# Centring instead of normalising three token tiles before the K and V projections, and moving two tile transposes from TensorE to DMA

## The chip, the cores and the metric

The kernel runs on one core of a Trainium2 chip. The metric is the time of one execution on the device in microseconds (us), as a median of several executions. The profile covers the kernel's own span, which is about 1.8 us shorter than that time.

## The reference, cut to what matters

```
xn  = layernorm(x)                       # x: 2048 tokens x 1024, no gain, no bias
q, k, v = xn @ wqkv                      # 32 heads of 32
phi(t) = where(t > 0, t + 1, exp(t)) + 1e-6
kv = sum over tokens of phi(k) v ;  z = sum over tokens of phi(k)
s  = (phi(q) kv / (phi(q) z + 1e-6)) @ wo
g  = silu( (silu(xn @ w_gate) * (xn @ w_up)) @ w_down )      # inner width 3584
out = x + s * g
```

The tokens are cut into 16 tiles of 128. The projections of this kernel take a tile with the model dimension on the partitions (the first axis of a tile, 128 long), so each normalised tile is transposed before K and V are projected from it.

## The kernel before

The kernel goes through stages: K and V of all tiles with the running state (up to about 128 us), Q and the attention result, and then the feed-forward part, which takes the most time. Only the first stage is rewritten. For each tile `i` the code has these helpers (shortened, `...` marks a cut):

```
NPE = 4                                   # tiles 0..3 are transposed by TensorE
def emit_stats(i): ...                    # VectorE: mean and variance
def emit_rstd_act(i): ...                 # ScalarE sqrt + VectorE reciprocal (tiles 0, 1)
def emit_rstd(i): ...                     # three small VectorE operations + Newton steps on GpSimd
def emit_N(i):                            # (x - mean) * rstd
    ...
    if i >= NPE:                          # ... and for tiles 4..15 the transpose, by DMA
        nc.sync.dma_start_transpose(out=xn_ap(...), in_=xn[:])
def emit_TR(i):                           # tiles 0..3: 8 TensorE transposes of 128x128, then a copy from PSUM
    ...
def emit_Bmm(i, c):                       # K (c = 0, 1) and V (c = 2, 3): 8 matmuls 128x512 into one PSUM bank
    ...
def emit_Bev(i, c):                       # K: ScalarE Exp and Relu, VectorE; V: ScalarE copy
    ...
def emit_C(i):                            # 8 matmuls: add tile i to the state
```

They are called in a fixed order, which is the order of instructions on each engine:

```
wps = psB.tile([P, CW], FP32, name="warm_ps", tag="B")          # psB has three PSUM banks
for k in range(NWARM):                                          # 11 matmuls on zeros
    nc.tensor.matmul(wps[:], lhsT=warm[:, 0:P], rhs=warm[:], start=True, stop=True)
emit_stats(0); emit_rstd_act(0); emit_N(0); emit_TR(0)
emit_stats(1); emit_rstd_act(1); emit_N(1)
emit_Bmm(0, 0); emit_TR(1); ...
```

PSUM is the memory in which the matmuls leave their results; here one result of 128x512 fills a bank. The loads of x and of the weights, and all transposing DMAs, are issued from one queue (SyncE) in program order. In the built program each transfer on it waits for the completion of the one eight before it.

Of the kernel before, what the change touches and what calls it, by code (L numbers as in the profile page):

```python
# [9 lines left out]
ACT = mybir.ActivationFunctionType  # L10
ALU = mybir.AluOpType
# [10 lines left out]
def kernel(  # L22
# [34 lines left out]
    NJ = (G + GPT - 1) // GPT  # L57
    EPS_LN = 1e-5
    EPS = 1e-6
    NPE = 4  # L60
    NWARM = 11
    NPREP = 13
    NWE = 7
# [37 lines left out]
    ident = persist.tile([P, P], BF16, name="ident")  # L101
    make_identity(nc, ident[:])
    ones = persist.tile([P, P], BF16, name="ones")
    nc.vector.memset(ones[:], 1.0)
    mkp = p12.enter_context(tc.tile_pool(name="mkp", bufs=1, reuse_waits="tile"))
    mask = mkp.tile([P, P], FP32, name="mask")
    nc.vector.memset(mask[:], 0.0)
    for j in range(HPG):
        nc.vector.memset(mask[j * DH:(j + 1) * DH, j * DH:(j + 1) * DH], 1.0)
    sel = mkp.tile([P, HPG], FP32, name="sel")  # L110
    nc.vector.memset(sel[:], 0.0)
    for j in range(HPG):
        nc.vector.memset(sel[j * DH:(j + 1) * DH, j:j + 1], 1.0)

    xn_blk_tiles = {b: xnp.tile([P, DC, TB], BF16, name="xnT", tag="xn8")
                    for p in range(NB // 2 - 1, -1, -1) for b in (2 * p, 2 * p + 1)}

    def xn_ap(dcs, tok):
        b = tok.start // TB
        return xn_blk_tiles[b][:, dcs, tok.start - b * TB:tok.stop - b * TB]  # L120
# [3 lines left out]
    wq_sb = w12.tile([P, DC, D], BF16, name="wq_sb")  # L124
    late = p12.enter_context(tc.tile_pool(name="late", bufs=1, reuse_waits="tile"))
    KVZ = late.tile([P, G, NDW], BF16, name="KVZ")
    s_dram = dram.tile([S, D], BF16, name="s_dram")
    HK = DC // 2
    TB2 = 2 * TB
# [12 lines left out]
        while phi_late:  # L142
            phi_late.pop(0)()

    def emit_phi(work, t_ps, dst, W, in_place=False, act=False):
        e_t = work.tile([P, W], FP32, name="e_t", tag="e_t")
        if act:
            nc.scalar.activation(out=e_t[:], in_=t_ps, func=ACT.Relu, scale=-1.0)
            nc.scalar.activation(out=e_t[:], in_=e_t[:], func=ACT.Exp, scale=-1.0)
            nc.scalar.activation(out=t_ps, in_=t_ps, func=ACT.Relu)  # L150
            phi_late.append(lambda: nc.vector.scalar_tensor_tensor(out=dst, in0=e_t[:], scalar=EPS, in1=t_ps,
                                                                   op0=ALU.add, op1=ALU.add))
            return
        nc.scalar.activation(out=e_t[:], in_=t_ps, func=ACT.Exp)
        if in_place:
            r = t_ps
            nc.vector.tensor_scalar(out=r, in0=t_ps, scalar1=0.0, scalar2=EPS, op0=ALU.max, op1=ALU.add)
        else:
            r_t = work.tile([P, W], FP32, name="r_t", tag="r_t")
            r = r_t[:]  # L160
            nc.scalar.activation(out=r, in_=t_ps, func=ACT.Relu)
            nc.vector.tensor_scalar(out=r, in0=r, scalar1=EPS, scalar2=None, op0=ALU.add)
        nc.vector.scalar_tensor_tensor(out=dst, in0=e_t[:], scalar=1.0, in1=r,
                                       op0=ALU.min, op1=ALU.add)
# [198 lines left out]
    with ExitStack() as p1:  # L363
# [39 lines left out]
        load_x(0)  # L403
        load_x(1)
        load_wkv(0, halves=2 if DC % 2 == 0 else 1)
        load_x(2)
        nx = 3
        for c in range(1, NCH):
            load_wkv(c)
        for i in range(nx, NT):  # L410
            load_x(i)
        def load_qo(wt, wv, c):
            nc.sync.dma_start(out=wt[:, :, c * CW:(c + 1) * CW], in_=wv[:, :, c * CW:(c + 1) * CW])

        for c in range(NCC):
            load_qo(wq_sb, wqkv_v, c)
        PRE_AT = {2: (5, 6), 3: (7, 8), 4: (9, 10), 5: (11, 12), 6: (13, 14), 7: (15,)}
        FMAX = nc.vector.BN_STATS_FMAX
        SCH = min(FMAX, D)
# [4 lines left out]

        grp_state = {}

        N_AT = {5: (4,), 6: (5,)}
        for k in range(6, NT):
            N_AT[k + 3] = (k,)

# [33 lines left out]
        def emit_rstd(gid, eng=None):  # L464
# [10 lines left out]
            for _ in range(NR_ITERS):  # L475
# [3 lines left out]
                                  op0=ALU.mult, op1=ALU.add)  # L479
                eng.tensor_tensor(out=y, in0=y, in1=w[:, 0:n], op=ALU.mult)  # L480

        def emit_norm(i, dst, cols=None):
            mv, rstd, k = ln_state[i]
            src = x_ap(i) if cols is None else x_ap(i)[:, cols]
            return nc.vector.tensor_scalar(out=dst, in0=src, scalar1=mv[:, k, 0:1], scalar2=rstd[:, k:k + 1],
                                           op0=ALU.subtract, op1=ALU.mult)
# [3 lines left out]
        def emit_N(i):  # L490
            xn = xnw.tile([P, D], BF16, name="xn", tag="xn")
            xn_tiles[i] = xn
            if i < 2:
                for hh in range(2):
                    cols = slice(hh * (D // 2), (hh + 1) * (D // 2))
                    emit_norm(i, xn[:, cols], cols=cols)
            else:
                emit_norm(i, xn[:])
            ln_state.pop(i)
            if i >= NPE:  # L500
                xn_tiles.pop(i)
                nc.sync.dma_start_transpose(out=xn_ap(slice(0, DC), slice(i * P, (i + 1) * P)), in_=xn[:])

        def emit_TR(i):
            tok = slice(i * P, (i + 1) * P)
            xn = xn_tiles.pop(i)
            nh = 2 if i < 2 else 1
            dch = DC // nh
            for hh in range(nh):
                tr_ps = psC.tile([P, dch, P], BF16, name="tr_ps", tag="C")  # L510
                for dc in range(dch):
                    nc.tensor.transpose(tr_ps[:, dc, :], xn[:, (hh * dch + dc) * P:(hh * dch + dc + 1) * P], ident[:])
                dst = xn_ap(slice(hh * dch, (hh + 1) * dch), tok)
                if i == 1 and hh == 0:
                    nc.vector.tensor_copy(out=dst, in_=tr_ps[:])  # L515
                else:
                    nc.scalar.copy(out=dst, in_=tr_ps[:])  # L517

        pkv_tiles = {}

        kv_banks = {}

        def emit_Bmm(i, c):
            tok = slice(i * P, (i + 1) * P)
            kv_ps = psB.tile([P, CW], FP32, name="kv_ps", tag="B")
            kv_banks[(i, c)] = kv_ps
            for dc in range(DC):
                mm = nc.tensor.matmul(kv_ps[:], lhsT=xn_ap(dc, tok), rhs=wkv_sb[:, dc, c * CW:(c + 1) * CW],  # L528
                                      start=(dc == 0), stop=(dc == DC - 1))
                if dc == 0 and c == 0:  # L530
                    marks[("B", i)] = mm

        def emit_Bev(i, c):
            kv_ps = kv_banks.pop((i, c))
            if i not in pkv_tiles:
                pk_sb = work.tile([P, D], BF16, name="pk_sb", tag="pk_sb")
                pkv_tiles[i] = (pk_sb, v_bufs[i % 2])
            pk_sb, v_sb = pkv_tiles[i]
            if c < NCC:
                emit_phi(phiw, kv_ps[:], pk_sb[:, c * CW:(c + 1) * CW], CW, in_place=i >= 9)  # L540
            else:
                vc = c - NCC
                nc.scalar.copy(out=v_sb[:, vc * GPC:(vc + 1) * GPC, 0:P],
                               in_=kv_ps[:].rearrange("p (g c) -> p g c", c=P))

        def emit_C(i):
            pk_sb, v_sb = pkv_tiles.pop(i)
# [7 lines left out]
        def ln_pre(i, eng=None):  # L555
            emit_stats(i)
            if i == grp_tiles(i)[-1]:
                emit_rstd(grp_of(i), eng)

        warm = work.tile([P, CW], BF16, name="warm", tag="warm")  # L560
        nc.vector.memset(warm[:], 0.0)
        wps = psB.tile([P, CW], FP32, name="warm_ps", tag="B")
        for k in range(NWARM):
            nc.tensor.matmul(wps[:], lhsT=warm[:, 0:P], rhs=warm[:], start=True, stop=True)  # L564
        stat_ps[0] = lambda: psC.tile([P, 1], FP32, name="st_ps", tag="C")[:]
        emit_stats(0)
        emit_rstd_act(0)
        emit_N(0)
        emit_TR(0)
        emit_stats(1)  # L570
        emit_rstd_act(1)
        emit_N(1)
        emit_Bmm(0, 0)
        emit_TR(1)
        ln_pre(2)
        emit_Bev(0, 0)
        emit_Bmm(1, 0)
        emit_Bmm(0, 1)
        emit_Bev(1, 0)
        emit_N(2)  # L580
        emit_Bev(0, 1)
        emit_Bmm(1, 1)
        emit_Bmm(0, 2)
        emit_Bev(1, 1)
        emit_Bev(0, 2)
        emit_TR(2)
        emit_Bmm(1, 2)
        emit_Bev(1, 2)
        ln_pre(3)
        emit_Bmm(2, 0)  # L590
        emit_Bmm(0, 3)
        emit_Bev(0, 3)
        emit_Bmm(1, 3)
        emit_Bev(1, 3)
        emit_N(3)
        ln_pre(4)
        emit_C(0)
# [28 lines left out]
        for i in range(2, NT):  # L626
            for c in range(NCH):
# [10 lines left out]
                    emit_C(i - 1)  # L638
                emit_Bev(i, c)
                if (i, c) == (2, 2):  # L640
                    emit_TR(3)
                if c % 2 == 1:
                    for k in N_AT.get(2 * i + c // 2, ()):
                        emit_N(k)
                        if 0 <= k - NPE < NCC:
                            load_qo(wo_sb, wo_v, k - NPE)
                    for k in PRE_AT.get(i, ())[c // 2:c // 2 + 1]:
                        ln_pre(k)
                if (i, c) in PREP_AT:
# [785 lines left out]
```

## Time and profile before

| | before |
|---|---|
| time, three runs | 758.15 us (758.14 to 758.18) |
| span of the profiled execution | 756.7 us |
| first projection / tile 1's first projection | 7.60 / 10.24 us |
| first matmul of Q | 127.8 us |
| first matmul of the feed-forward part (output `xb`) | 245.3 us |

The profiled execution is one of 758.5 us, a little slower than the three runs.

The prediction below shows the page's head, the waits and the first 11 us. Two further views: the first is the timeline around tile 3's transpose on TensorE. Its columns are the start and the length in us, then engine, line, operation, output and input, and how many instructions are grouped.

```profile
29.15 0.61 PE L512 MATMUL tr_ps<-ident,xn 128*128 128x128 bf16 x8
29.60 3.62 PE L528 MATMUL kv_ps<-wkv_sb,xnT 128*128 128x512 bf16 x15
```

The eight transposes hold the stream from 29.15 to 29.60, which is 0.45 us, and the projections go on at once. That is what a tile's transpose costs on TensorE.

The second is the DMA view from 30 to 36 us. Each number is a slice of 0.15 us. It holds the kernel's first transposing DMA, that of tile 4, issued at 32.53. The lower row gives its time from issue to landing (3.2 us).

```profile
GB/s 348 341 362 335 362 335 301 198 116 41 27 20 27 20 27 20 7 0 55 0 0 0 0 0 0 55 205 213 222 207 208 210 179 169 105 92 191 130 116 307
...
xnT<-xn SPq DMA_TRANSPOSE x1, 3.2
```

About 1.25 us pass before the first bytes, the data take some 1.4 us at about 210 GB/s, and the rest of the 3.2 us is the time after the last bytes.

### The profile page before, as it was taken

What the parts mean: (1) busy time and instruction counts of PE and PEld (TensorE: products, weight loads), DVE (VectorE), ACT (ScalarE), POOL (GpSimd) and SP (SyncE); (2) the same over time, 40 slices, a digit from 0 to 9 for tenths busy, and PEclk for the clock granted to TensorE, in tenths of its full rate; (3) what the DMA queues carried; (4) which work ended last, traced back from release to release, by engine and by line L of the source; (5) the groups of instructions that cost most, each with busy time, mean ns of one, the idle gap of its engine ahead of it and who ended that gap; (6) DMA issues with size and microseconds to landing.
All of it is one profiled execution on the core that took longest, in us unless ns stands there. A gap on an engine that the chain in (4) does not pass through costs nothing.

```text
span 756.7 us, 10426 instructions
## 1 busy us (share of the span) xinstructions
PE 746.6 (99%) x3662; PEld 349.0 (46%) x3731; DVE 558.5 (74%) x1031; ACT 376.3 (50%) x526; POOL 278.4 (37%) x352
## 2 busy tenths in 40 slices
PE   8999999999999999999999999999999999999997
PEld 4544544454454444444444444444444444444443
DVE  6687787896697788888889775368676777787335
ACT  5677776889956565666659311132322223211122
POOL 2444799998540276868585000100000000200000
PEclk9999999999999999999999999999999999999999
DMA  9968799879679668878799236398644445530824
GB/s 316 295 149 146 223 334 300 302 137 307 201 180 298 229 217 292 309 268 312 278 329 408 86 121 239 124 377 321 229 174 167 167 168 173 180 133 15 283 83 135
DMA packets 105845, 170.30 MB, mean 225 GB/s; under 512 B 34816, under 2 KB 82176, under 8 KB 95168
## 3 DMA queue, kind: packets, MB, share of 16 engines
q1 hardware_dynamic: 100144, 144.99, 59.3%
q0 software_dynamic: 4208, 22.15, 7.5%
q10 hardware_dynamic: 1440, 2.49, 0.9%
q8 instruction: 29, 0.48, 0.3%
q14 instruction: 24, 0.20, 0.1%
HBM read 111.67 MB, written 50.59 MB: 214 GB/s over the span
## 4 chain that ended last, share of the span: by engine, by line
PE 97%; DVE 1%; ACT 1%; issue 1%; ACTq 0%; DVEq 0%
PE zw L939 26%; PE kv_ps L528 15%; PE xb L939 13%; PE dzw L1124 12%; PE yb L939 6%; PE q_ps L183 6%; PE dx L1124 6%; PE dy L1124 3%; PE fx L790 3%; PE s_ps L748 2%; PE kvz L550 1%; PE nd L717 1%; PE df L1124 1%; PE warm_ps L564 1%; DVE w_sb L283 0%
## 5 line engine op out<-in xcount | busy, mean ns | idle before, releaser
L939 PEld LDWEIGHTS <-w_sb 128*128 128x128 f16 (+1 forms) x1568 | 152.1, 98 | 182.7
L939 PE MATMUL xb<-xnT,w_sb 128*128 128x512 bf16 x420 | 113.3, 379 | 1.5
L528 PE MATMUL kv_ps<-wkv_sb,xnT 128*128 128x512 bf16 x499 | 112.9, 379 | 1.1 <-DVE xnT L515 0.3
L939 PE MATMUL zw<-xnT,w_sb 128*128 128x512 bf16 x448 | 105.8, 379 | 0.0
L939 PE MATMUL zw<-S,w_sb 128*128 128x512 f16 x448 | 105.8, 379 | 0.0
L295 POOL TENSOR_TENSOR w_sb<-w_sb 128x512 f16<-128x512 bf16 x42 | 50.2, 1195 | 95.7 <-DVE w_sb L283 51.3
L260 ACT ACTIVATE w_sb<-w_sb 128x2048 bf16<-128x2048 bf16 x42 | 79.9, 1902 | 4.4 <-DMA w_sb<-in_B_w_up_dram 4.4
L1124 PE MATMUL dx<-w_sb,hT 128*128 128x512 bf16 x202 | 76.6, 379 | 0.3
L528 PEld LDWEIGHTS <-xnT 128*128 128x128 bf16 x512 | 48.4, 98 | 55.9 <-ACT xnT L517 0.8
L1124 PEld LDWEIGHTS <-hT 128*128 128x128 bf16 (+1 forms) x462 | 44.7, 98 | 52.4
L183 PE MATMUL q_ps<-xnT,wq_sb 128*128 128x512 bf16 x249 | 58.0, 379 | 0.4
L1015 ACT ACTIVATE sg<-cg 128x1024 bf16<-128x1024 f32 x28 | 29.6, 1057 | 57.4 <-DVE cg L1008 57.4
L939 PE MATMUL yb<-S,w_sb 128*128 128x512 f16 x224 | 57.4, 378 | 0.1
L1124 PE MATMUL dzw<-w_sb,hT 128*128 128x512 f16 (+1 forms) x190 | 57.0, 379 | 0.0
L1008 DVE SCALAR_TENSOR_TENSOR cg<-zw,rc_all,s 128x1024 f32<-128x1024 f32 x28 | 35.9, 1284 | 25.5 <-PE zw L939 13.8
L967 DVE SCALAR_TENSOR_TENSOR s<-yb,rc_all,s 128x512 f32<-128x512 f32 x42 | 31.5, 749 | 28.1 <-ACT s L966 28.1
L296 POOL TENSOR_TENSOR w_sb<-w_sb 128x512 f16<-128x512 bf16 x42 | 50.5, 1201 | 3.3
L1064 POOL TENSOR_TENSOR hs<-hT 128x512 f16<-128x512 bf16 x2 | 2.5, 1250 | 132.6 <-ACT sg L1015 132.6
L298 POOL TENSOR_TENSOR w_sb<-w_sb 128x512 f16<-128x512 bf16 x42 | 50.2, 1196 | 0.0
L297 POOL TENSOR_TENSOR w_sb<-w_sb 128x512 f16<-128x512 bf16 x42 | 50.2, 1195 | 0.0
L1098 POOL DMA_DIRECT2D out_dram<-io x16 | 8.7, 542 | 101.9 <-DVE io L1097 101.6
L966 ACT ACTIVATE s<-xb,rcl 128x512 f32<-128x512 f32 x14 | 9.6, 687 | 65.3 <-PE xb L939 65.3
(179 smaller groups left out, 1187.4 us busy)
## 6 DMA issues: line engine op xcount, KB each, us to landing
w_sb<-pk_g SPq DMA_DIRECT2D x27, 1024.0 KB, 6.3
pk_g<-w_sb SPq DMA_DIRECT2D x14, 1024.0 KB, 5.0
w_sb<-wd SPq DMA_DIRECT2D x14, 1024.0 KB, 6.0
w_sb<-pk_u SPq DMA_DIRECT2D x14, 1024.0 KB, 5.0
pk_u<-w_sb POOLq DMA_DIRECT2D x13, 1024.0 KB, 5.3
w_sb<-wd SPq DMA_DIRECT2D x14, 768.0 KB, 4.8
w_sb<-in_B_w_gate_dram SPq DMA_DIRECT2D x14, 512.0 KB, 6.7
w_sb<-in_B_w_down_dram SPq DMA_DIRECT2D x28, 256.0 KB, 4.9
```

What stands on the lines that cost most here:

```text
L183: nc.tensor.matmul(q_ps[:], lhsT=wq_sb[:, dc, g * P:(g + 1) * P], rhs=xn_ap(dc, btok), start=(dc == 0), stop=(dc == DC - 1))
L260: nc.scalar.activation(out=junk, in_=raw_view(key, t), func=ACT.Square, accum_out=asum[:])
L295: nc.gpsimd.tensor_tensor(out=T1, in0=b12, in1=b11, op=ALU.subtract)
L296: nc.gpsimd.tensor_tensor(out=T2, in0=b22, in1=T1, op=ALU.subtract)
L297: nc.gpsimd.tensor_tensor(out=T3, in0=b22, in1=b12, op=ALU.subtract)
L298: nc.gpsimd.tensor_tensor(out=T4, in0=b21, in1=T2, op=ALU.subtract)
L528: mm = nc.tensor.matmul(kv_ps[:], lhsT=xn_ap(dc, tok), rhs=wkv_sb[:, dc, c * CW:(c + 1) * CW], start=(dc == 0), stop=(dc == DC - 1))
L939: mm = nc.tensor.matmul(out, lhsT=lhs(k), rhs=rhs(k), start=(first and k == 0), stop=(k == HK - 1), skip_group_check=True)
L967: nc.vector.scalar_tensor_tensor(out=s2[:], in0=y_[:], scalar=rc, in1=s1[:], op0=ALU.mult, op1=ALU.add)
L1008: nc.vector.scalar_tensor_tensor(out=d12, in0=zw[:], scalar=rc, in1=s2[:, None, :].to_broadcast([P, 2, TB]), op0=ALU.mult, op1=ALU.add)
L1015: nc.scalar.activation(out=sg[:, 1:3, :], in_=cf[:], func=ACT.Silu)
L1124: nc.tensor.matmul(out, lhsT=lhs, rhs=rhs, start=first, stop=lastk, skip_group_check=True)
```

## The change

It shortens the way to the first projection and takes work off TensorE.

- Tiles 0 to 2 are only centred for K and V. (x - mean) W times 1/std is the same as the projection of the normalised tile, and 1/std belongs to a token, which is a partition of the result. So 1/std can be the `scale` of the ScalarE instruction that empties the bank, and the projection doesn't wait for it.
- Tile 1's TensorE transposes go in halves between the projections of tile 0.
- Tiles 2 and 3 are transposed by DMA instead of TensorE.
- Q and the feed-forward part need the normalised tiles, so tiles 0 to 2 are normalised again later and transposed by DMA.
- x2 is loaded behind the second chunk of weights, x3 behind tile 2's transpose, and the loads of the Q weights are issued later.
- The warm-up reads other memory, whose memset comes first on VectorE, and writes two PSUM banks in turn.

```diff
-    NPE = 4
+    NPE = 2
+    NDF = 3
@@ phi and the V evacuation
-        nc.scalar.activation(out=e_t[:], in_=t_ps, func=ACT.Exp)
+        nc.scalar.activation(out=e_t[:], in_=t_ps, func=ACT.Exp, scale=scale)   # rstd_of[i] for i < NDF
...
@@ loads
-        load_x(2)
         for c in range(1, NCH):
             load_wkv(c)
-        for i in range(nx, NT):
-            load_x(i)
+            if c == 1:
+                load_x(2)
...
+        def emit_center(i):
...
+                nc.vector.tensor_scalar(out=xn[:, cols], in0=x_ap(i)[:, cols], scalar1=mv[:, k, 0:1], scalar2=None,
+                                        op0=ALU.subtract)
+            if i >= NPE:
+                emit_DT(i)
+        def emit_DT(i):
+            nc.sync.dma_start_transpose(out=xn_ap(slice(0, DC), slice(i * P, (i + 1) * P)), in_=xn_tiles.pop(i)[:])
...
-        wps = psB.tile([P, CW], FP32, name="warm_ps", tag="B")
+        wps = [psB.tile([P, CW], FP32, name="warm_ps", tag="B") for _ in range(2)]
@@ the order
         emit_stats(0)
+        emit_center(0)
         emit_rstd_act(0)
-        emit_N(0)
-        emit_TR(0)
+        emit_TR(0, 0, nc.scalar)
+        emit_TR(0, 1, nc.scalar)
         emit_stats(1)
+        emit_center(1)
+        emit_Bmm(0, 0, range(6))
+        emit_TR(1, 0, nc.vector)
         emit_rstd_act(1)
-        emit_N(1)
-        emit_Bmm(0, 0)
-        emit_TR(1)
+        emit_Bmm(0, 0, range(6, DC))
+        emit_TR(1, 1, nc.scalar)
...
+        emit_stats(2)
+        emit_center(2)
+        load_x(3)
...
+        for i in range(4, NT):
+            load_x(i)
...
+        emit_N(0)
         emit_N(3)
```

`emit_N(0)` normalises tile 0 again and issues its transposing DMA, which nothing needs before Q at about 128 us. `emit_N(3)` does the same for tile 3, which TensorE needs at about 29 us. The one for tile 0 stands first.

## The prediction

> **What bounds the kernel now.** I read the page's busy shares first, then the chain that ended last, then the waits of the matmul engine, then the first 34 us as a timeline. The first lines are from the page (busy us, share, count; then the chain's shares by engine).
>
> ```profile
> span 756.7 us, 10426 instructions
> PE 746.6 (99%) x3662; PEld 349.0 (46%) x3731; DVE 558.5 (74%) x1031; ACT 376.3 (50%) x526; POOL 278.4 (37%) x352
> ...
> PE 97%; DVE 1%; ACT 1%; issue 1%; ACTq 0%; DVEq 0%
> ```
>
> TensorE is busy for 746.6 of 756.7 us, and 97% of the chain is TensorE. So only two things pay: fewer TensorE instructions, or fewer gaps between them. Its whole list of waits above 0.2 us is four lines (us in total, times, longest):
>
> ```profile
> PE warm_ps L564 <- DVE warm L561: 1.5, 1, 1.5
> PE nd L264 <- ACT w_sb L260: 0.3, 1, 0.3
> PE kv_ps L528 <- DVE xnT L515: 0.3, 1, 0.3
> PE kv_ps L528 <- ACT xnT L517: 0.3, 1, 0.3
> ```
>
> Three of the four are in the first 11 us, the part that the change rewrites. The chain of waits there (start, us, what):
>
> ```profile
> 1.49 4.87 PE warm_ps L564 x11
> 6.36 0.57 PE tr_ps L512 x4
> 6.93 0.02 issue
> 6.96 0.59 ACT xnT L517
> 7.55 0.05 issue
> 7.60 1.90 PE kv_ps L528 x8
> 9.50 0.24 PE tr_ps L512 x4
> 9.74 0.02 issue
> 9.76 0.44 DVE xnT L515
> 10.20 0.05 issue
> 10.24 3.19 PE kv_ps L528 x14
> ```
>
> The 11 warm-up matmuls compute nothing, so the head is really paced by the statistics of token tile 0. The timeline shows these ahead of the first transpose (start, us, engine, what):
>
> ```profile
> 3.69 1.29 DVE L447 BATCH_NORM_STATS2 stats<-xp 128x6 f32<-128x512 bf16 x2 [1.47 <-DMA xp<-in_A_x_dram]
> 5.01 0.21 DVE L448 BATCH_NORM_AGGREGATE mv<-stats 128x2 f32<-128x12 f32 x1
> 5.32 0.29 ACT L460 ACTIVATE rstd<-mv,eps_ln 128x1 f32<-128x1 f32 x1 [3.29 <-DVE mv L448]
> 5.64 0.16 DVE L461 RECIPROCAL rstd<-rstd 128x1 f32<-128x1 f32 x1 [0.43 <-ACT rstd L460]
> 5.84 0.74 DVE L485 TENSOR_SCALAR xn<-xp,mv,rstd 128x512 bf16<-128x512 bf16 x2
> ```
>
> The trip to ScalarE and the reciprocal keep the normalisation from starting at about 5.26 (aggregate's end 5.22 plus a hop of 0.04); it starts at 5.84.
>
> **What the Trainium skill says.** (1) "TensorE: Matmul & The Clock Gate", Back-to-back issue gap, gives 55.6 and 215.7 ns between warm matmuls of 128 and 512 columns. The trace agrees: 8 transposes delay the stream by 0.45 us (56 ns each), and a group of 8 projections takes about 1.73 us (216 ns each). The 379 ns in the page's rows is latency, and I do not use it. (2) The same page, Part 1, has TensorE cold at half clock until some 3.4 us of activity. The warm-up spacing here, 0.43 us, agrees with a cold array, and the projections at 7.60 run at the warm rate. (3) "ScalarE: Activation LUTs", What ACT_TABLE_LOAD costs: each per-partition pointer operand adds about 93 ns. The trace has about 0.60 us for the Exp evacuation without a pointer and 0.67 for the one of s_ps, which has one; I take +0.07 to +0.09. (4) "Advanced Engine Details and Errata", X-Bar Transpose (TRN2), calls transposing DMAs as fast as regular ones. Here it is slower: around the first one (33.8 to 35.2 us) the queue moves some 210 GB/s, against about 385 when it loads x. So its 0.26 MB cost about 1.3 us of queue instead of 0.68.
>
> **The change, part by part.** *Start.* Centring needs only the mean, so it begins at 5.26 instead of 5.84: 0.58 us. The first half ends at about 5.63 and its transpose can start at 5.73, against 6.31. Warm-up must not be in the way: its memset now stands first on VectorE, so it starts 0.32 earlier (the memsets ahead of it took 0.84 to 1.16), and its last matmul gives way at about 5.7 to 5.9. I take 0.5 us of gain: first projection at 7.1 instead of 7.60.
>
> *Tile 1.* Its first transposes now go after 6 of the 8 projections of tile 0, its second after the last 2. VectorE: reciprocal 6.0, statistics 6.2 to 7.7, centring 7.75 to 8.5. TensorE: 6 projections 7.1 to 8.4, 4 transposes, copy on VectorE at about 8.4+0.42 = 8.82 to 9.25, meanwhile 2 projections and 4 transposes up to 9.35. So tile 1 starts at about 9.35 against 10.24: 0.9 in all up to here, which includes the 0.5.
>
> *Transposes of tiles 2 and 3.* 16 matmuls leave TensorE, 0.45 us per tile: 0.9 us. The wait on the copy of tile 3, about 0.1 ahead of its projections at 31.3, goes too.
>
> Sum: 0.9 + 0.9 + 0.1 = **1.9 us**. Tile 3 then starts at 9.35 + 8 groups x 1.73 + two state updates 1.07 + 3 x 1.73 = 29.4, against 31.3.
>
> *Added beside the path.* Tiles 0 to 2 are normalised again for Q and the feed-forward: 3 x 0.55 us on VectorE (74% busy) and three transposing DMAs, about 4 us of queue, at 21 to 35 us. The scaled evacuations are 18 x 0.08 = 1.4 us on ScalarE, half of it by 20 us. The wq loads move from 21 us to about 50, where the windows show the DMA at 50 to 79%, and Q reads them at 128. All of these have slack of tens of us, apart from the following.
>
> **The rivals.** *A. The DMA transpose of tile 3 comes late and takes the place of what was removed.* The queue is saturated from 2.4 to about 31 us in the trace before. Through weight chunk 3 it has the same 4.98 MB as before, whose last piece landed at 4.8 + 12.4 = 17.2. Then tile 2's transpose (1.3 us; data to 17.6), 13 x tiles (13 x 0.68 = 8.8, to 26.4), then the transposes of tile 0 (to 27.7) and tile 3 (to 29.1), landing at about 29.5. TensorE wants it at 29.4. This is a tie: I expect a stall between 0 and 0.8 us, and give 0.2 to the mean. The other way into it, tile 3's statistics, is: x3 lands 19, statistics and the three small operations to 20.7, the Newton steps on GpSimd 3.3 to 4.4 us, issue at 25 to 26; it is ahead of the queue's data. A stall over 2 us would need the queue to hold transposes much longer.
>
> *B. PSUM banks.* Three banks, freed by ScalarE after a table load of 1.28 us that cannot start before the last copy (10.57 before, 10.1 now): Exp 11.4, Relu to 12.6 or 12.7. The fourth group wants its bank at 9.35 + 2 x 1.73 = 12.8. There is a margin of 0.1, a tie again, worth at most 0.3. Later banks have 0.6, if x2 is not over a us late.
>
> *C. x2 and weight chunk 1.* Chunk 1 landed at about 2.75 + 8.4 = 11.15 before, with x2 in front of it; the second group of tile 0 now wants it at 11.1. Behind chunk 1, x2 (0.68 us of queue) lands at about 11.1 and chunk 1 at 10.4. So this part only prevents a new wait. Tile 2 is then centred at 13.3, transposed by about 18, and wanted at 23.2 - 1.73 = 21.4: 3 us of slack.
>
> *D. The gain is taken back later.* At 165 to 173 us the chain runs for a moment through weight preparation: DVE w_sb L283 (3.67 us), then ACT w_sb L260, with a TensorE wait of 0.3. If that ran on its own clock, up to 1.9 us would vanish. Against it: the chain enters that stretch from a TensorE matmul at 160.07, and every preparation step stands in program order between TensorE's evacuations, so it should shift with TensorE. After it no wait over 0.2 us is left up to the end.
>
> *E. The clock gate.* If the earlier, two-bank warm-up left the array cold for longer, some groups would run at 427 ns a matmul, 1.7 us lost a group. Little speaks for it: just as many warm-ups, and fewer gaps after them.
>
> **Range and chances.** 758.15 - 1.9 = 756.25. A costs 0.2 on average and B 0.05, so 756.5. With no stall and a hidden gap more it could be 755.9; with A at 1 us or D taking half, 757.5. 2% is 15 us; nothing here is that large in either direction.
>
> **What would show each step.** First centring at 5.2 to 5.3 and first projection at about 7.1; tile 1 at about 9.35; 16 fewer tr_ps matmuls; no TensorE wait on chunk 1; tile 2's first projection at 21.4; tile 3's at 29.4 to 30, with any wait put down to a DMA on xnT (A). Wait on ScalarE or a longer gap near 12.8 is B. Whether TensorE is still 1.7 to 1.9 us ahead at 128 us (first q_ps at 127.8 before) and after 175 us tells D. The prediction is wrong if the first stretch ends with less than 1 us gained, if a DMA transpose is over 1.5 us late, or if the lead at 128 us is not in the end time.

## The result, and the profile after

| | before | after |
|---|---|---|
| time, six runs of the same rounds | 758.14 us (758.00 to 758.19) | 758.65 us (758.07 to 759.74) |
| span of the profiled execution | 756.7 us | 756.3 us |
| tile 1's first projection | 10.24 us | 9.39 us |
| first matmul of Q | 127.8 us | 128.4 us |
| first matmul of the feed-forward part | 245.3 us | 245.2 us |

The ratio of after to before is 1.0008, with a 95% interval from 0.9995 to 1.002: no difference. Ratios here are the mean time of one kernel's runs over that of the other's runs of the same rounds, so they are not quite the ratio of the medians that I quote. The predicted 756.5 us, with a range from 755.9 to 757.5, is missed by 2.15 us. The profiled executions took 758.5 us before and 758.07 us after, which is the fastest of the six, so their spans differ the other way from the medians.

The page of the kernel after has these lines in place of those shown of before:

```profile
span 756.3 us, 10420 instructions
PE 745.0 (99%) x3647; PEld 348.0 (46%) x3715; DVE 558.2 (74%) x1034; ACT 376.1 (50%) x524; POOL 279.8 (37%) x352
...
PE 95%; DMA 2%; DVE 1%; issue 1%; POOL 0%; SPq 0%; ACT 0%
```

TensorE has fewer instructions and 1.6 us less busy time, as intended. (The count falls by 15 rather than 16; a few matmul records can be missing from a trace.) But the chain that ended last now runs through DMA for 2% of the span, where no DMA showed before. (By line, the page gives 2% to the loads of x that the statistics of a tile need, and 1% to a transpose, both rounded.) The waits of TensorE say what it costs:

```profile
PE kv_ps L533 <- DMA xnT<-xn: 1.6, 1, 1.6
PE warm_ps L569 <- DVE KVZ L118: 1.2, 1, 1.2
PE q_ps L186 <- ACT v_sb L549: 0.7, 1, 0.7
PE kv_ps L533 <- ACT xnT L519: 0.4, 1, 0.4
```

Before, no wait outside the first 11 us was longer than 0.3 us. Now there are two: 1.6 us for a transposing DMA and 0.7 us at the start of Q. The timeline of the kernel after shows how the first 34 us went:

```profile
5.17 0.61 DVE L489 TENSOR_SCALAR xn<-xp,mv 128x512 bf16<-128x512 bf16 x2
7.17 1.47 PE L533 MATMUL kv_ps<-wkv_sb,xnT 128*128 128x512 bf16 x6 [0.41 <-ACT xnT L519]
...
9.39 13.99 PE L533 MATMUL kv_ps<-wkv_sb,xnT 128*128 128x512 bf16 x63
...
13.31 1.34 SPq L495 DMA_TRANSPOSE xnT<-xn  x1
14.70 7.16 SPq L396 DMA_DIRECT2D xp<-in_A_x_dram  x13
...
22.29 12.27 SPq L495 DMA_TRANSPOSE xnT<-xn  x4
24.14 5.34 PE L533 MATMUL kv_ps<-wkv_sb,xnT 128*128 128x512 bf16 x23
...
31.07 1.90 PE L533 MATMUL kv_ps<-wkv_sb,xnT 128*128 128x512 bf16 x8 [1.59 <-DMA xnT<-xn]
```

Down to 24.14 everything is where the prediction has it. The 63 matmuls from 9.39 are unbroken, so tile 2, transposed by DMA, was not waited for. Then the group that starts at 24.14 ends, and tile 3 waits 1.59 us. The chain of waits of the kernel after names the transfer:

```profile
24.59 0.55 DVE xn L500
...
25.17 5.86 DMA xnT<-xn
31.02 0.05 issue
31.07 1.90 PE kv_ps L533 x8
```

Tile 3 is normalised at 25.14 and its transpose is issued at 25.17, inside the predicted 25 to 26. It then takes 5.86 us to land, nearly twice what the first transpose of the kernel before took on an idle queue. The DMA view from 26 to 30 us (slices of 0.1 us) shows what it waited behind:

```profile
GB/s 430 430 348 190 289 294 289 289 110 20 20 20 21 41 20 20 20 20 23 18 18 18 148 287 289 289 272 285 289 287 289 292 289 287 289 269 111 0 0 0
...
xnT<-xn SPq DMA_TRANSPOSE x1, 5.9
```

This row is read from left to right in four pieces. The x loads end at about 26.3, where the prediction had 26.4. Then data at another rate, some 290 GB/s, flow for half a microsecond: the first part of the transposes. From 26.9 to 28.2 almost nothing moves: about 20 GB/s, as in the tail of the kernel before, although two transposes are queued. From 28.2 to 29.7 both transposes move together at about 289 GB/s. Adding up the slices at 289 or so, before and after the pause, gives some 0.53 MB, which is just the two tiles of 0.26 MB each, so both tiles' data are through at 29.7. Even then tile 3's transfer counts as landed only at 31.02, 1.3 us later.

A sixteenth of the 350 to 390 GB/s that the loads reach is 22 to 24 GB/s. The Trainium skill ("DMA: Bandwidth & Descriptors", Why a DMA increments its semaphore by 16 and not by 1) says that a DMA runs on up to 16 engines that finish independently. So one engine of 16 that still works off its share of the loads would fit the 20 GB/s.

The views don't show this, but the packed trace of each run keeps sixteen landing signals for every transfer on this queue, and every packet. They agree. Up to the x load that landed at 22.20 the sixteen signals of a load come within 0.2 us. In each of the next six loads fifteen come together and one comes 1.4 to 1.5 us later: 22.87 and 24.34 in the first, 26.29 and 27.69 in the sixth. (All sixteen of the very last load come at 28.3 to 28.4.) The late part's packets of x go on to 27.9. The packets of the transposes stand still from 26.8 until then, and 22 of them took 1.4 us each, where some 18 ns is usual. Of tile 3's transpose fifteen parts have landed by 30.17, and the sixteenth comes at 31.02.

The lag of the x loads begins after a 16 KB transfer of the instruction queue, which took 1.09 us from 21.73; the one of tile 3 comes with an 8 KB transfer of such a queue at 29.6. The same order of events is in the profiles of all versions that send two transposes behind the x loads. That these transfers cause the lags fits, but no run moved them, so it is not shown.

### The profile page after: what moved, and what is told of

It is laid out like the page before. It is cut to its first block, busy times and chain, and to the rows that moved or that the text cites. A ratio compares the mean times of both kernels' runs of the same rounds, so it can differ in the third digit from the quotient of the medians. Undisturbed runs are those within 1.5% of the kernel's fastest.

```text
span 756.3 us, 10420 instructions
## 1 busy us (share of the span) xinstructions
PE 745.0 (99%) x3647; PEld 348.0 (46%) x3715; DVE 558.2 (74%) x1034; ACT 376.1 (50%) x524; POOL 279.8 (37%) x352
## 4 chain that ended last, share of the span: by engine, by line
PE 95%; DMA 2%; DVE 1%; issue 1%; POOL 0%; SPq 0%; ACT 0%
PE zw L953 26%; PE xb L953 13%; PE kv_ps L533 12%; PE dzw L1138 12%; PE q_ps L186 7%; PE yb L953 6%; PE dx L1138 6%; PE dy L1138 3%; PE fx L804 3%; PE s_ps L762 3%; DMA xp<-in_A_x_dram 2%; PE nd L731 1%; PE kvz L557 1%; DMA xnT<-xn 1%; PE df L1138 1%
## 5 line engine op out<-in xcount | busy, mean ns | idle before, releaser
L1029 ACT ACTIVATE sg<-cg 128x1024 bf16<-128x1024 f32 x28 | 29.6, 1057 | 57.5 <-DVE cg L1022 57.5
L981 DVE SCALAR_TENSOR_TENSOR s<-yb,rc_all,s 128x512 f32<-128x512 f32 x42 | 31.4, 748 | 30.2 <-ACT s L980 30.2
```

The costliest lines, as they stand in the source:

```text
L981: nc.vector.scalar_tensor_tensor(out=s2[:], in0=y_[:], scalar=rc, in1=s1[:], op0=ALU.mult, op1=ALU.add)
L1029: nc.scalar.activation(out=sg[:, 1:3, :], in_=cf[:], func=ACT.Silu)
```

## The experiments

The first question was whether tile 3's wait comes from the queue or from the tile's own statistics, and what it is worth. The second was what makes Q wait. The third, which came up on the way, was why some executions of the changed kernel end late although they were ahead at 245 us. The letters in the expectations are the rivals of the prediction and the names that the theories had. Edits are against the changed kernel unless I say otherwise. Every run gave correct results.

| run | what it is | median (range), us | ratio to before, 95% |
|---|---|---|---|
| e1_tile3_first | tile 3's DMA issued ahead of tile 0's | 758.19 (757.58 to 758.75) | 0.9998 [0.9985, 1.001] |
| e2_x_late | x8 to x15 loaded later | 759.29 (757.01 to 760.59) | 1.001 [0.9996, 1.0023] |
| e3_warm1 | one warm-up bank | 758.71 (758.44 to 759.13) | 1.0007 [0.9994, 1.0021] |
| e4_first_warm1 | e1 and e3 together | 757.12 (756.77 to 759.69) | 0.9991 [0.9978, 1.0003] |
| f1_first_warm3 | e1 with three warm-up banks | 757.21 (757.06 to 757.54) | 0.9987 [0.9974, 0.9999] |
| f2_warm3 | three warm-up banks alone | 759.03 (757.96 to 760.24) | 1.0008 [0.9995, 1.0022] |
| f3_after_again | the change, unedited | 758.34 (758.09 to 758.99) | 1.0002 [0.9989, 1.0014] |
| f4_tile3_pe | tile 3 back on TensorE | 757.00 (756.65 to 758.07) | 0.9985 [0.9972, 0.9997] |
| g1_pe3_warm3 | f4 with three warm-up banks | 756.88 (756.79 to 757.72) | 0.9984 [0.9972, 0.9997] |
| g2_x2_first | f1 with x2 ahead of weight chunk 1 | 756.51 (755.96 to 757.12) | 0.9979 [0.9965, 0.9992] |
| k1_g2_upfirst | g2, two later loads exchanged | 757.15 (756.59 to 758.49) | 0.9989 [0.9975, 1.0003] |
| k2_after_upfirst | the change, the same exchange | 758.70 (758.00 to 759.47) | 1.0004 [0.9991, 1.0016] |
| m1_before_dup5 | the kernel before, five DMAs twice | 758.91 (758.43 to 759.42) | 1.0005 [0.9992, 1.0019] |
| m2_g2_dup3 | g2, three DMAs twice | 757.36 (755.96 to 758.25) | 0.9985 [0.9973, 0.9998] |

Each of these is a median of five. The letter e, f, g, k or m marks what ran together on one chip; the kernel before had medians of 758.28, 758.13, 758.23, 758.33 and 758.33 beside them, of nine runs each.

### Is it the queue that makes tile 3 wait?

**e1_tile3_first** exchanges the order of the two transposing DMAs and nothing else.

```diff
-        emit_N(0)
+        emit_N(0, dt=False)      # normalise tile 0, no DMA yet
         emit_N(3)
+        emit_DT(0)
```

> The change, with tile 3's transposing DMA issued ahead of tile 0's (nothing else moved). Theory A (tile 3's transpose lands late because it stands behind the x loads and tile 0's transpose in one saturated queue; it landed at 31.0 us and TensorE wanted it at 29.4): tile 3's transpose lands some 1.3 us or more sooner, before 29.8, the TensorE wait of 1.6 us on it falls to 0.4 or less, tile 3's projections start at 29.4 to 29.9, and the time falls by 1.0 to 1.6 us against the change, if the later wait of 0.7 us on the last V evacuation stays. Rival I (the transpose is late because its own input is late: statistics and the Newton steps on GpSimd): its issue stays at 25.2 and it lands at 31 as before, no gain. Rival D (what is gained here is taken back later): tile 3 starts at 29.5, and the end still is within 0.3 us of the change.

The wait on tile 3 is gone. The timeline of this run has one unbroken group where the changed kernel had 23 matmuls and a wait:

```profile
24.37 7.34 PE L534 MATMUL kv_ps<-wkv_sb,xnT 128*128 128x512 bf16 x32
```

Tile 3's transpose is issued at 25.65 and lands after 4.1 us instead of 5.9. At 245 us this run is 1.2 us ahead of the changed kernel (243.97 against 245.21). Its end time gains less than the expected 1.0 to 1.6 us (758.19 against 758.65, in other rounds); a part of the reason comes below.

**e2_x_late** leaves the order as it is, and takes eight x loads out of the queue ahead of the two transposes.

```diff
-        for i in range(4, NT):
+        for i in range(4, 8):
             load_x(i)
...
         emit_N(3)
+        for i in range(8, NT):
+            load_x(i)
```

> The change, with the loads of token tiles 8 to 15 moved behind the transposes of tiles 0 and 3 in the queue. Theory A: the queue is short when tile 3's transpose is issued at 25.2, so it lands after about 3.2 us, at 28.4, the TensorE wait on it is gone, tile 3 starts at 29.4, and the time falls by about 1.6 us against the change; its spread over executions (758.07 to 759.74) shrinks to that of the kernel before (0.2 us). Rival I (late input): still issued at 25.2 and landing at 31, no gain. If A is right and a later statistics step now waits for x8 and later tiles, a new wait appears on VectorE after 36 us, with none on TensorE.

Tile 3 doesn't wait here either. The DMA view of this run from 22 to 29 us (slices of 0.175 us) shows the two transposes with nothing ahead of them:

```profile
GB/s 0 0 0 0 0 67 211 218 215 212 206 189 166 15 0 0 0 0 0 0 0 0 0 0 0 47 205 215 217 211 209 193 178 142 70 0 222 386 398 398
...
xnT<-xn SPq DMA_TRANSPOSE x2, 3.1
```

They are issued at 21.76 and 25.29 and land 3.1 us later. For the first, 1.2 us pass before the data, 1.4 us with data, and about 0.5 us after the last bytes (landing at 24.83). Tile 3 was normalised at 25.27, no earlier than in the changed kernel. So late input is not the reason; what differs is what the queue holds: 3.1 us with nothing ahead, 4.1 behind the x loads (e1), 5.9 behind the x loads and another transpose. The pause is absent here (in e1 the packets of the transposes still stand still for 0.6 us): all sixteen parts of the x loads ahead had landed by 21.73, before the first byte of a transpose. The version itself is no use. The later loads push back tile 4's transpose, and TensorE waits 1.48 us for that one at 38.2 and 0.44 us once more at 46.2, so the wait has only moved. The expected narrow spread didn't come either (757.01 to 760.59).

**f4_tile3_pe** gives tile 3 back to TensorE and keeps the rest of the change.

```diff
-        emit_N(3)
+        emit_N(3, dt=False)
...
                 if (i, c) == (2, 2):
                     emit_N(1)
+                    emit_TR(3, 0, nc.scalar)
+                    emit_TR(3, 1, nc.scalar)
```

> The change with tile 3 transposed by TensorE again (two halves, ScalarE copies), its DMA transpose dropped; all else as the change. Theory A: no wait on a DMA of xnT at tile 3, 0.45 us of transposes and up to 0.3 of waiting for the copy instead of 1.6: 0.8 to 1.2 us under the change. Rival D (nothing gained before 31 us reaches the end): no difference over 0.3.

It costs the 0.45 us of the eight transposes again and removes a wait of 1.6 to 1.9 us. Its median is 757.00, against 758.34 of the unedited change on the same chip (**f3_after_again**, where tile 3 waited 1.91 us): 1.3 us better, near the 1.45 us that 1.9 - 0.45 gives. The closeness is partly luck: in the profiles f4 is 1.0 us ahead of f3 at the first Q matmul (127.23 against 128.22), as it has a new wait of 0.47 us for a later tile's transpose at 44.6, and f3's profile has a late wait of 0.8 us at 328 us that f4's doesn't have.

> The change itself once more, for its spread and a second profile. If the late transpose of tile 3 is steady, the wait is again 1.3 to 2 us and the time 758.0 to 759.7. If the head is governed by the landing of x0 and of the second half of weight chunk 0 (0.4 to 0.7 us of wait in three of four experiments so far), the first projection and tile 1's start move by up to 0.8 us from the first profile.

### What makes Q wait?

In the changed kernel the first matmul of Q waits 0.68 us, with ScalarE's copy of the last V group ending just before. In the built programs the banks show why: with one or two banks taken by the warm-up, the rotation of the three banks puts the last V group of the stage into bank 3, and the first Q group wants just that bank. In the kernel before, the last V group is in bank 5. My first guess was that the second warm-up bank had shifted the rotation by one, so that one bank would put it right. **e3_warm1** tests that, and **e4_first_warm1** adds e1's order.

```diff
-        wps = [psB.tile(...) for _ in range(2)]
+        wps = [psB.tile(...) for _ in range(1)]
```

> The change, with the warm-up in one PSUM bank instead of two. Theory W (the second bank turns the rotation of three banks by one, so that the first Q group takes the bank that the last V evacuation is still reading): the TensorE wait of 0.7 us of the first q_ps on the V evacuation at 127.8 is gone, the head of the kernel is unchanged (first projection at 7.2, the wait on tile 3's transpose about 1.6), the time falls by 0.3 to 0.7 us. Rival (the wait comes from TensorE or ScalarE standing in another order, not from the bank): the wait of 0.7 stays.

> Both: tile 3's transpose ahead of tile 0's, warm-up in one bank. If A and W are right and their gains add: about 1.6 + 0.6 = 2.2 us off the change, some 756.3, that is 1.7 to 1.9 us below the kernel before, as the prediction's sum had it. Rival D: lead of 1.9 us at 127 us, but less than 1 us of it in the end time.

The guess was wrong: the Q wait is 0.7 us in both. (e3 waits 1.86 us for tile 3, and e4, with e1's order, 0.20 us, so that order alone leaves hardly any slack either.) The changed order of the projections had moved the rotation too. With three warm-up banks the built program has the last V group in bank 5 again. **f1_first_warm3** and **f2_warm3** do that, with and without e1's order.

> Tile 3's transpose ahead of tile 0's, warm-up in three PSUM banks. In the built programs the first Q group takes bank 3; the last V evacuation reads bank 5 in the kernel before, bank 3 in the change and in the variant with one warm-up bank (which is why that one kept the wait), and bank 5 in this variant. Theory W2 (same bank, so the first Q group waits for the evacuation): the wait of 0.7 us of q_ps on v_sb is gone, no wait above 0.3 us on tile 3's transpose, and the time is 0.6 us under that of e1_tile3_first: 757.0 to 757.6, or 756.5 if no new wait falls in. Rival (the order of the engines makes the wait): 0.7 stays.

> The change with three warm-up banks alone. W2: the wait of q_ps on v_sb gone, the wait on tile 3's transpose still 1 to 2 us; 0.6 us under the change: about 758.0. Rival: 0.7 stays, time as the change.

The wait disappears from both. The timelines of the changed kernel and of f1 around the start of Q:

```profile
127.76 0.60 ACT L549 ACTIVATE v_sb<-kv_ps 128x512 bf16<-128x512 f32 x1 [0.46 <-PE st_ps L267]
128.41 1.89 PE L186 MATMUL q_ps<-xnT,wq_sb 128*128 128x512 bf16 x8 [0.68 <-ACT v_sb L549]
```

```profile
125.71 1.02 PE L186 MATMUL q_ps<-xnT,wq_sb 128*128 128x512 bf16 x4
...
125.88 0.60 ACT L550 ACTIVATE v_sb<-kv_ps 128x512 bf16<-128x512 f32 x1 [0.46 <-PE st_ps L267]
```

In f1 Q starts while ScalarE still copies the last V group; in the changed kernel it starts after that. But the wait is worth much less than its 0.68 us. From the first Q matmul to the first feed-forward matmul, all eight profiles with this wait need 116.80 to 116.85 us (after, f3, e1 to e4, f4, k2). The six without it need 117.4 to 117.8 (f1, f2, g1, g2, k1, m2), and so do four of the five profiles of the kernel before. The kernel before shows where in part: it has a wait of 0.3 us on ScalarE at 173 us, which the prediction's list shows and the changed kernel's doesn't have. One could think that ScalarE has the same backlog either way and that TensorE pays for it once, at 128 us or after it. But that is not shown: the fifth profile of the kernel before (**h1_before**) needs 116.84 us with neither wait, and f1 and g2 need 117.4 us with no wait over 0.12 us. In any case f2, which only removes the wait and was expected at about 758.0, gains nothing: 759.03 us, against 758.34 of f3 on the same chip.

f1 and f2 differ in nothing but the order of the two DMAs, and ran on the same chip. This is the cleanest pair. The timeline of f2, then of f1:

```profile
24.14 5.34 PE L533 MATMUL kv_ps<-wkv_sb,xnT 128*128 128x512 bf16 x23
30.92 1.90 PE L533 MATMUL kv_ps<-wkv_sb,xnT 128*128 128x512 bf16 x8 [1.44 <-DMA xnT<-xn]
```

```profile
23.93 7.16 PE L534 MATMUL kv_ps<-wkv_sb,xnT 128*128 128x512 bf16 x31
```

The medians are 759.03 and 757.21 us. Issuing tile 3's DMA ahead of tile 0's is worth 1.8 us here, of which the wait of 1.44 is most, and none of the five runs of one overlaps with those of the other.

### The rest of the change, and the best version

**g1_pe3_warm3** is f4 with three banks, **g2_x2_first** is f1 with x2 loaded ahead of the second weight chunk, as before the change:

```diff
+        load_x(2)
         for c in range(1, NCH):
             load_wkv(c)
-            if c == 1:
-                load_x(2)
```

> Tile 3 transposed by TensorE and warm-up in three banks: both waits that the change brought in are taken away. From f4_tile3_pe (757.0, with 0.7 us of wait on v_sb left): 756.3 to 756.6, that is 1.5 to 1.8 us under the kernel before, if the wait at about 327 us (0.6 to 0.9 in five of nine profiles) does not fall in; 0.6 more if it does. If what is gained before 128 us were taken back later as a rule, it would stay at 757.

> f1_first_warm3 with x2 put ahead of weight chunk 1 again, as in the kernel before: what the order of x2 is worth by itself. Step C of the prediction: chunk 1 lands 0.7 us later, at about 11.1, and the second group of tile 0 wants it at 10.8 to 11.1: a TensorE wait on wkv_sb of 0 to 0.5 us near 11 us, tile 2's statistics 0.7 us earlier, and the time 0 to 0.5 us above f1_first_warm3 (757.2). Rival: x2 earlier brings tile 2, its transpose and the x loads earlier, and the time falls.

g1 is no better than f4 was (756.88 and 757.00, on different chips), which agrees with what f2 says of the banks. g2 is the fastest kernel, 756.51 us, and 1.7 us below the kernel before on the same chip. The weight chunk now lands 0.35 us too late, as the prediction's rival C has it, and TensorE waits for it at 10.94. From tile 1's first projection to the first Q matmul g2 needs 0.4 us more than f1 (116.95 against 116.53), which is this wait. But g2's profile started 0.5 us earlier (8.68 against 9.18), so it reaches Q at 125.63 and f1 at 125.71, and the end times show no loss. As g2 is the best of many versions, some of its lead may be chance: k1 and m2 below have the same start and came to 757.15 and 757.36 us. What sets f1's profile apart from g2's comes next.

### Why some executions lose up to 1 us near 327 us

f1's profile is 2.2 us ahead of the first profile of before at 245 us (243.13 against 245.29), but only 1.1 us ahead at the first matmul that writes `df`, near the end (745.40 against 746.53). g2's lead is 2.2 us at both. Most of the difference is a TensorE wait of 0.9 us at 326 us in f1, put down to ScalarE, which g2 doesn't have. ScalarE itself waited for a 512 KB slice of the up-projection's weights. These are the timeline lines of ScalarE in f1 and then in the kernel before, for the statistics of that slice:

```profile
320.85 1.91 ACT L263 ACTIVATE w_sb<-w_sb 128x2048 bf16<-128x2048 bf16 x1 [5.30 <-DMA w_sb<-in_B_w_up_dram]
```

```profile
317.62 1.90 ACT L260 ACTIVATE w_sb<-w_sb 128x2048 bf16<-128x2048 bf16 x1
```

It lands 12.2 us after its issue in f1, and 6.7 us after it in this profile of the kernel before. Over all profiles:

| kernels | profiles | issue to landing of this slice, us | TensorE wait near 327 us |
|---|---|---|---|
| before (with m1) | 6 | 6.7 to 7.5 | none |
| the change and its variants, landing up to 10.3 | 9 | 8.1 to 10.3 | none |
| the change and its variants, landing 11.9 or more | 5 | 11.9 to 12.5 | 0.6 to 0.9 |

The five are f3, e1, e2, f1 and f2. The first profile of the changed kernel is not among them (10.1 us). So the wait comes and goes between executions of one kernel, and it makes a part of the spread of the changed kernel's times (758.07 to 759.74). Four looks at the kernel before made sure that its short landing was no chance of one profile (7.5, 7.3, 7.1 and 6.9 us):

> The kernel before, unchanged, for a second profile. If the wait of TensorE near 327 us on ScalarE, which is held up by the landing of a w_up slice, is the chip's and not the change's, it appears here in some profiles too: time 758.5 to 758.6 with it, 758.0 to 758.1 without. First projection 7.2 to 7.6 whatever the landing of x0, as weight chunk 0 lands at 7.5 to 8.1.

> The kernel before once more, third profile, as h1_before: with the wait near 327 us 758.5 to 758.6, without it 758.0 to 758.1.

> The kernel before, a fourth profile. If the late w_up slice is the chip's own jitter, a wait near 327 us may appear here with 758.5 or more; if it goes with the change, none, and 757.9 to 758.2.

> The kernel before, a fifth profile, with the same two outcomes as h3_before: a wait near 327 us and 758.5 or more, or none and 757.9 to 758.2.

Their times were 757.88, 757.98, 758.39 and 758.71 us, in an unknown state, as single looks are. The last two lie above the 757.9 to 758.2 us that were expected without the wait, so the kernel before too has a spread that this wait doesn't explain.

Two theories of the cause were tried, and both fell. The first: the slice is queued behind a gate slice, so issuing it ahead of that one would bring it in earlier. **k1_g2_upfirst** and **k2_after_upfirst** exchange the two in g2 and in the changed kernel.

```diff
-            w_seq.append((p, "g", fg))
-            w_seq.append((p, "u", fg))
+            for kd in ("ug" if (p, fg) == (passes[0], NFG - 4) else "gu"):
+                w_seq.append((p, kd, fg))
```

> g2_x2_first with the w_up slice of pair 10 (issued at about 309 us) ahead of the 1 MB gate slice of the same pair. Theory U (the wait near 327 us comes from that slice landing late): it lands in 5 to 9 us, ScalarE does not wait for it over 3 us, no TensorE wait near 327, the runs gather within 0.5 us (755.96 to 757.12 before), median 756.0 to 756.4. Rival (the wait comes from something else, or the gate slice now lands too late): the wait near 327 stays or another comes, median 756.5 or above.

> The change itself with the same swap. U: no wait near 327 us; the waits on tile 3's transpose (1.4 to 1.9) and on the last V evacuation (0.7) stay; median 758.0 to 758.2 instead of 758.34 to 758.65, spread smaller. Rival: as the change.

It landed after 10.3 us in k1 (8.3 in g2) and 8.4 in k2 (10.1 and 12.2 in the unedited change). No wait shows in either profile, but the times are no better (757.15 and 758.70), and the landing stays longer than in the kernel before.

The second: the change has issued five more transfers on the queue by then, so the eight-deep window of completions stands at another place. **m1_before_dup5** issues five transposing DMAs of the kernel before twice, and **m2_g2_dup3** three more in g2, so that the total is a multiple of eight again.

```diff
+                if 7 <= i < 12:      # m1; m2: 9 <= i < 12
+                    nc.sync.dma_start_transpose(out=xn_ap(...), in_=xn[:])
```

> The kernel before with the transposing DMAs of tiles 7 to 11 issued twice (same data, same place): five more transfers, nothing else. Theory N (the number of earlier transfers sets how the later ones share the queues): the w_up slice of 309 us lands in 8 to 12.5 us, a TensorE wait near 327 us falls into some executions, median 758.3 to 758.9. Rival (something else in the change does it, or chance): it lands in 6.7 to 7.5 us, no wait near 327, time as the kernel before. The repeats themselves cost some 1.3 us of queue each between 45 and 75 us, where nothing waits for them.

> g2_x2_first with the transposing DMAs of tiles 9 to 11 issued twice: eight more transfers than the kernel before, so the same phase of the eight semaphores. Theory N: the slice lands in 6.7 to 7.5 us, no wait near 327, runs within 0.5 us of each other, median 755.9 to 756.4. Rival: lands in 8 us or more as in g2_x2_first (756.51, 755.96 to 757.12), spread as there.

The landing stayed at 7.1 us in m1 and at 10.1 us in m2: each as its own family, not as the phase of the window would have it. (m1's median of 758.91 is above the 758.33 beside it, but not clear of the noise; its profile has a wait of 1.1 us on VectorE in the Q stage.) What makes this slice land later in all versions of the change stays open. The built programs have it at the same address and in the same order, and the transfers around it are the same. But one of these is issued at another moment, a rival that no run tested: GpSimd's 1 MB store of `pk_u`. In the six profiles of the kernel before it is issued 0.8 to 1.4 us after the slice (308.97 and 310.34 in the first), in the versions of the change between 0.9 us before it and 1.2 us after it (308.51 and 308.17 in f1). In all nine profiles in which the two are issued within 0.4 us of each other the slice takes 9.9 us or more, in the other eleven 9.8 or less.

## Why the prediction was wrong, point by point

The table puts the mean of the five profiles of the kernel before beside the mean of the two of the unedited change, leg by leg. The means are needed since the landing of the first x half moves the head by some tenths in both kernels (tile 1's first projection at 9.67 to 10.24 before, 8.88 and 9.39 after). A leg ends where TensorE starts the thing named. The predicted column charges the mean stall.

| leg | before | after | difference | predicted |
|---|---|---|---|---|
| start to tile 1's first projection | 10.00 | 9.14 | -0.86 | -0.9 |
| to the first Q matmul | 117.62 | 119.18 | +1.56 | -0.8 |
| to the first feed-forward matmul | 117.39 | 116.82 | -0.57 | 0 |
| to the first `df` matmul, near the end | 501.31 | 501.72 | +0.41 | 0 |
| to the end of the span | 10.19 | 9.89 | -0.30 | 0 |

**The start** was right. Centring began at 5.17 (predicted 5.26), the first projection came at 7.17 (7.1), tile 1 at 9.39 (9.35). The scaled Exp took 0.69 us, inside the 0.67 to 0.69 that the step gives.

**The transposes of tiles 2 and 3 leaving TensorE** were right as well: the eight transposes per tile are gone, and f4 pays 0.45 us to have one tile's back. Tile 2's landing, predicted at about 18, came at 18.1, and nobody waited.

**Rival A is the step that failed.** The prediction named the mechanism and gave its sign: "This is a tie: I expect a stall between 0 and 0.8 us, and give 0.2 to the mean." It was 1.59 and 1.91 us in the two profiles of the change, and e1, e2, f4 and the pair f1 and f2 show that the place in this queue makes it, and not late input. TensorE did want tile 3 when predicted (24.14 + 5.34 = 29.48, against 29.4), and the data of fifteen of the sixteen parts of the x loads ended when predicted (26.3, against 26.4). What failed is the time from there to the landing of the two transposes. I took 1.3 us of queue for each, one after the other, and 0.4 us to land: 29.1, and landed at 29.5. Measured: the last part of the x loads went on to 27.9, and the transposes' data, standing still meanwhile, were through at 29.7. The pause of 1.3 us was partly made good by a rate of 289 instead of 210 GB/s. Fifteen parts of tile 3's transpose landed 0.5 us after the data, about as assumed, but the sixteenth came at 31.02, 1.3 us after them, and the wait is for all. So 0.6 us of the error of 1.5 lie in the pause, and 0.9 in the landing, nearly all of it in one late part. I had worked from the one transpose in the trace that had an idle queue, and used its time as if it held behind a full one.

The way out was in reach of the prediction. It put the two transposes down in the order "tile 0 and tile 3", and called their sum a tie, but didn't remark that tile 0's isn't needed for another 100 us.

**The bank rotation was missed.** Rival B looked for ties among the three banks in the head only, and there no wait came. The wait of 0.68 us at 128 us is new, but most of it comes back by 245 us: +0.68 in the second leg, -0.57 in the third. Net it is about 0.1 us. It would have been wrong to add it to the loss, though it is the second largest line in the list of waits.

**Rival D did not happen as told.** The lead that a version has at 128 us is not taken back at 165 to 173 us: f1 and g2 are 1.9 and 2.0 us ahead of the mean of the kernel before there (125.71 and 125.63 against 127.62), and 1.9 us ahead at 245 us (243.13 and 243.07 against 245.01). A part is taken back later, near 327 us, in some executions.

**Rivals C and E** were right. No wait on chunk 1 came with x2 behind it, though the end times don't show that this order is worth anything. (e1, e2 and e3 waited 0.4 to 0.7 us for the second half of chunk 0 instead, at 7.7 to 8.1 us.) The projections ran at their warm rate from the start (the 63 records of eight groups from 9.39 span 13.99 us, 219 ns for each of 64).

**What the prediction took from "TensorE: Matmul & The Clock Gate".** The 55.6 and 215.7 ns stand there under "Wait — 56ns, not 53.3ns?". The section that the prediction named gives about 81 and 131 ns for a stream with weight loads, which the trace doesn't show (56 and 216 ns). The 3.4 us of Part 1 are too short: the transposes still went at some 107 ns each, twice their later 56, up to 6.4 us in the kernel after, 5.2 us after the first warm-up matmul.

The sum for the end: -0.86 for the start and -0.9 for the transposes give -1.76; the stall adds 1.75 on average, the banks about 0.1, and the wait near 327 us 0.41 in the mean of two profiles. That is +0.5 us at the first `df` matmul. The change then gains 0.30 us up to the end, for which I have no cause, so these profiled executions differ by +0.24 us in the mean (758.53 against 758.29). The medians of the rounds differ by +0.5; the two profiles of the change alone are 0.9 us apart, so the sum can't be tested more finely than this. For g2, where the order and the banks are mended and the profile shows no late wait, the first two terms are left, -1.76 us, and -1.7 was measured: 756.51 us, the predicted figure for the change, which the change as written didn't reach. Some luck is in this too, as k1 and m2 show.

## What to carry to other kernels

When work moves from a busy engine to a transfer, ask when the transfer lands behind what is queued ahead of it, not how long it takes alone; and put transfers into the queue by the time at which they are needed. Where a prediction finds a tie between a transfer and the engine that bounds the kernel, its cost isn't symmetric, since an early landing gains nothing, so the mean should lean to the late side. And a new line in the list of waits is not yet a loss: follow a milestone further down, as the engine may have paid the same time somewhere else before.

## What the Trainium skill lacked or had wrong

- "Advanced Engine Details and Errata", X-Bar Transpose (TRN2), calls transposing DMAs as fast as regular ones and expects 350 to 400 GB/s. Here one alone moves at about 210 GB/s and two in the queue together at about 289, against 385 to 398 for the x loads. "DMA: Bandwidth & Descriptors", Latency and other measured facts, has 261 GB/s for a non-contiguous case, which is nearer.
- The page "DMA: Bandwidth & Descriptors" gives a fixed cost of about 2.0 us of a DMA, most of it after the last byte, for another way of issuing (Anatomy of one DMA — SWDGE (gpsimd) path). For the transposes issued by SyncE here it was 1.2 us before the data and 0.5 us after them in e2_x_late, and 1.3 us after them for the second of two that ran together. No page that I read has a number for how much later a transpose lands behind other transfers: 3.1 us alone, 4.1 behind x loads, 5.9 behind x loads and another transpose.
- No page that I read has a number for one part in sixteen of a queue's transfers falling behind. Here it was 1.4 to 1.5 us in the x loads from 22.9 us on, after a 16 KB transfer of the instruction queue that took 1.09 us; transposes behind them stood still for the tail of about 20 GB/s (26.9 to 28.2). The kernel before has such a tail from 31.4 to 32.4.
- No page has the spread of one and the same load between executions: 6.7 to 7.5 us for the weight slice at 309 us in the kernel before, 8.1 to 12.5 us in the versions of the change, with a cause that stayed open.
